# The last layer of a DCN cross kernel: row tails ahead of the sums, two row tiles through a DMA transpose, one semaphore for the last stores

## The chip, the cores and the metric

One core of a Trainium2 chip runs the kernel. Its engines are TensorE (PE in the profile, PEld for its weight loads), VectorE (DVE), ScalarE (ACT), GpSimd (POOL) and SyncE (SP), which here issues DMAs and waits. The metric is the time of one execution on the device in microseconds (us), lower is better; the number for a kernel is the median of its runs.

## The reference

```python
B, F, D, L = 4096, 26, 16, 6          # Din = 416
def reference(x0, ws, bs):            # x0 [4096, 416], ws [6, 416, 416], bs [6, 416], bf16
    x = x0
    for l in range(ws.shape[0]):
        x = x0 * (x @ ws[l] + bs[l]) + x
    return x
```

Six cross layers, each a 416x416 matrix product, an elementwise product with the input and a sum. Since every layer multiplies by the same x0, x after any layer is x0 times a running sum: x = x0 * (1 + sum over the layers of (x_l W_l + b_l)).

## The kernel before, in words

The 4096 rows are cut into four blocks of 1024 rows (`s`, size `SB`), each of two halves of 512 (`h`). Within a block the activations are kept transposed: features on the 128 partitions, rows along the free dimension. The 416 features are three chunks of 128 (`c`, `m`, `k`) and a tail of 32 columns.

PSUM holds the running sum of a block over all its layers: bank `3h + m` for half `h` and output chunk `m`, and banks 6 and 7 (`T_BANK`) for the tail. It is not reset between layers. `main` (mains) multiplies a 128-feature chunk of x with the weights, as four matmuls of 32 columns that run beside one another; `tail_rows` adds what the 32 tail features contribute, `tail_outs` makes the tail's own outputs. After each layer `leave` (L437, DVE) forms x = x0 * (PSUM + constant) for the next layer into `xT_sb`, where the constants (`cb_sb`) are one plus the summed biases. `leave_tail` does the same for the tail: ACT copies PSUM to `t32_sb` (L447), POOL multiplies (L460), and ACT and POOL make copies that the row-packed tail matmuls need (L424, L426).

`Plan` records every operation with what it reads and writes, in the order in which the Python loops name them. Each engine runs its operations in that order; where one needs a result of another engine or of a DMA, it waits on a semaphore. An operation that reads a PSUM bank is ordered behind earlier readers of that bank. Each DMA group has one semaphore, named by the `dma=` argument; a wait on it is for all DMAs of the group. Where an operation needs several semaphores, extra wait instructions stand ahead of it in its queue.

For blocks 0 to 2, `transpose_block` (L474) turns the finished block back with DMA transposes on SP's queue (L477, L482), and `store_block` (L484), called at L585 for `l == 3` of the next block, lets POOL place the tail columns (L488) and SP store the rows (L501).

The last layer of the last block (`s = 3`, `l = 5`) is computed the other way round, with rows on the partitions, so that no transposing is needed behind it. It has eight row tiles (`j`) of 128 rows, one PSUM bank each (`ROW_BANKS`, tile 0 in bank 6, 1 in 7, 2 to 7 in banks 0 to 5):

- `keep_sum` (L466) saves the running sums plus constant of layers 0 to 4 as bf16 into `sS_sb`, before the banks are taken over: half 0 on ACT, half 1 on ACT, ACT and DVE. `bt` and `st` (L588, L593, POOL) do that for the tail.
- `row_main` (L626) computes x W for a tile; tiles 0 to 3 "narrow", as four 32-column matmuls each, tiles 4 to 7 whole.
- `row_sums` (L636) adds the kept sums, turned by a multiplication with the identity.
- `row_tails` (L648) adds what the tail features and tail sums contribute, to all eight tiles at once, four tiles in each of two groups; for tiles 4 to 7 it is the first write of the bank.
- `finish` (L670) multiplies by x0 (`xr_sb`, loaded by rows): on DVE straight from PSUM (L674), or by an ACT copy (L681) and a POOL product (L685) for tiles 1 and 3.
- `store_rows` (L689) stores one or two tiles; six stores on SP's and ACT's queues, each with a semaphore of its own. SP then waits for all of them and for the earlier blocks' stores.

The order of the end: mains of tiles 0 to 3, sums of tiles 0 to 3, tails, `finish` of 0 to 3, and then main, sums and `finish` of each of 4 to 7.

Of the kernel before, what the change touches and what calls it, by code (L numbers as in the profile page):

```python
# [6 lines left out]
FP32 = mybir.dt.float32  # L7
ALU = mybir.AluOpType
# [110 lines left out]
def bass_standalone__dcn_v2_cross__recsys_kernel(  # L119
# [6 lines left out]
    B, D = x0.shape  # L126
    L = ws.shape[0]
    NC = 3
    DF = 128 * NC
    DR = D - DF  # L130
    assert DR == 32
    SB = 1024
    NS = B // SB
    H = SB // 2
# [5 lines left out]
    CH = range(NC)  # L140

    with ExitStack() as es:

        def sb(name, shape, dt=BF16):
            return es.enter_context(nc.sbuf_tensor(name, shape, dt))

        w_sb = sb("w_sb", [128, L, NC, D])
# [5 lines left out]
        xr_sb = sb("xr_sb", [128, JS, D])  # L153
        x0T_sb = sb("x0T_sb", [128, NC, B])
# [4 lines left out]
        sS_sb = sb("sS_sb", [128, NC, SB])  # L159
        st_sb = sb("st_sb", [128, G])  # L160
        f32_sb = sb("f32_sb", [128, 2, D], FP32)
        xo_sb = sb("xo_sb", [128, NS - 1, NC, SB])
        xot_sb = sb("xot_sb", [128, NS - 1, G])
        ot_sb = sb("ot_sb", [128, NS - 1, 2, 128])
# [16 lines left out]
        P = Plan()  # L181
# [4 lines left out]
        def bank(h, m):  # L186
            return NC * h + m


        def load(queue, dst, src, name, writes):  # L190
            P.add(queue, lambda e: e.dma_start(dst, src), writes=writes, dma=name)
# [76 lines left out]
            ), reads=[("ones",)], writes=[("u",)],  # L268
        )
        P.add("gpsimd", lambda e: e.memset(wc_sb[:, :, :], 0.0), writes=[("wc", "wt%d" % i) for i in range(3)])  # L270

        def replicate():
            for g, eng in ((1, "gpsimd"), (3, "scalar"), (2, "gpsimd")):
# [33 lines left out]
        def src_main(s, l):  # L307
            if l == 0:
                return x0T_sb, s * SB
            return xT_sb[:, l % 2], 0  # L310
# [116 lines left out]
                P.add(eng, fn, reads=[key], parts=[key + ("swapped",)], shifts=True)  # L427


        def leave(s, l, h, c):  # L430
            if l == L - 1:
                dst, key = xo_sb[:, s, c, h * H:(h + 1) * H], ("xo", s, c, h)
            else:
                dst, key = xT_sb[:, (l + 1) % 2, c, h * H:(h + 1) * H], ("xT", (l + 1) % 2, c, h)
            o = s * SB + h * H
            P.add(
                "vector", lambda e: e.scalar_tensor_tensor(  # L437
                    out=dst, in0=ps[:, bank(h, c), :], scalar=cb_sb[:, c, l:l + 1], in1=x0T_sb[:, c, o:o + H],
                    op0=ALU.add, op1=ALU.mult,
                ), reads=[("ps", bank(h, c)), ("cb",), ("x0T", s, c, h)], writes=[key],  # L440
            )
# [22 lines left out]
                swap(xt_sb[:, (l + 1) % 2], key, ("scalar", "gpsimd", "scalar", "gpsimd"))  # L464

        def keep_sum(h, c, eng):  # L466
            o, i, b = sS_sb[:, c, h * H:(h + 1) * H], ps[:, bank(h, c), :], cb_sb[:, c, L - 1:L]
            if eng == "scalar":
                fn = lambda e: e.activation(out=o, in_=i, func=ACTF.Identity, bias=b)  # L469
            else:  # L470
                fn = lambda e: e.tensor_scalar_add(o, i, b)
            P.add(eng, fn, reads=[("ps", bank(h, c)), ("cb",)], writes=[("sS", c, h)])

        def transpose_block(s):  # L474
            for c in CH:
# [76 lines left out]
        for s in range(NS):  # L552
            for l in range(L):
                ending = s == NS - 1 and l == L - 2
                if s == NS - 1 and l == L - 1:
                    break
                if s == 0 and l == 0:
                    for k in CH:
                        for part in range(2) if k == 0 else (None,):
                            for m in CH:  # L560
                                main(s, l, 0, m, k, part)
                        if k == 1:
                            tail_in()
                            bias_sums()
                    tail_rows(s, l, True)
                    for c in CH:
                        leave(s, l, 0, c)
                    tail_outs(s, l, False)
                else:
                    for m in CH:  # L570
                        for k in CH:
                            main(s, l, 0, m, k)
                    tail_rows(s, l, l == 0)
                    for c in CH:
                        leave(s, l, 0, c)
                    tail_outs(s, l, False)
                if s == 0 and l == 1:
                    corner(2, L, "wt2")
                leave_tail(s, l, not ending)
                if l == 2 and 0 < s < NS - 1:  # L580
                    place_tail(s + 1)
                if s == 0 and l == 0:
                    corner(1, 2, "wt1")
                if l == 3 and s > 0:
                    store_block(s - 1)  # L585
                if ending:
                    P.add(
                        "gpsimd", lambda e: e.tensor_tensor(  # L588
                            out=bt_sb[:, :], in0=cb_sb[:, NC, L - 1:L], in1=cb_sb[:, NC, L - 2:L - 1], op=ALU.subtract
                        ), reads=[("cb",)], writes=[("bt",)],  # L590
                    )
                    P.add(
                        "gpsimd", lambda e, t=t32_sb[:, l % 2, :]: e.tensor_scalar_add(st_sb[:, :], t, bt_sb[:, :]),  # L593
                        reads=[("t32", l % 2), ("bt",)], writes=[("st",)],
                    )
                    for c in CH:
                        keep_sum(0, c, "scalar")
                for m in CH:
                    for k in CH:
                        main(s, l, 1, m, k)  # L600
                    leave(s, l, 1, m)
                if ending:
                    for c in CH:
                        keep_sum(1, c, ("scalar", "scalar", "vector")[c])
            if s < NS - 1:
                transpose_block(s)
            if s < NS - 2:
                load_transposed(s + 2, 0, SB)
                load_last_columns(s + 2)
            if s == NS - 2:  # L610
                load("sync", xr_sb[:, :, :], x0_v[:, (NS - 1) * JS:NJ, :], "xr", [("xr",)])


        s, l = NS - 1, L - 1
        ROW_BANKS = (6, 7, 0, 1, 2, 3, 4, 5)
        src, off = src_main(s, l)
        srct, tkey = src_tail(s, l)

        def row_mm(pe, dst, lhsT, rhs, start, narrow):
# [6 lines left out]
        def row_main(j, start, narrow):  # L626
            b, h = ROW_BANKS[j], j // 4
            for k in CH:
                P.add(
                    "tensor", lambda pe, k=k: row_mm(  # L630
                        pe, ps[:, b, 0:D], src[:, k, off + j * 128:off + (j + 1) * 128], w_sb[:, l, k, :],
                        start and k == 0, narrow,
                    ), reads=[("w", l), src_key(s, l, k, h)], adds=[("ps", b)],
                )
# [34 lines left out]

        def finish(j, by_pool):  # L670
            b, jj = ROW_BANKS[j], (NS - 1) * JS + j
            if by_pool is None:
                P.add(
                    "vector", lambda e: e.tensor_tensor(  # L674
                        out=o_sb[:, jj, :], in0=ps[:, b, 0:D], in1=xr_sb[:, j, :], op=ALU.mult
                    ), reads=[("ps", b), ("xr",)], writes=[("ol", j)],
                )
                return
            t = f32_sb[:, by_pool, :]
            P.add(  # L680
                "scalar", lambda e: e.activation(out=t, in_=ps[:, b, 0:D], func=ACTF.Copy),  # L681
                reads=[("ps", b)], writes=[("f32", by_pool)],
            )
            P.add(
                "gpsimd", lambda e: e.tensor_tensor(out=o_sb[:, jj, :], in0=t, in1=xr_sb[:, j, :], op=ALU.mult),  # L685
                reads=[("f32", by_pool), ("xr",)], writes=[("ol", j)],
            )

        def store_rows(queue, a, b):  # L689
            ja = (NS - 1) * JS  # L690
            P.add(
                queue, lambda e: e.dma_start(out_v[:, ja + a:ja + b, :], o_sb[:, ja + a:ja + b, :]),
                reads=[("ol", j) for j in range(a, b)], writes=[("outl", a)], dma="outl%d" % a,
            )

        for j in range(4):
            row_main(j, True, True)
        for j in range(4):
            row_sums(j, True)
        row_tails()  # L700
        finish(0, None)
        finish(1, 0)
        finish(2, None)
        finish(3, 1)
        for j in range(4, 8):
            row_main(j, False, False)
            row_sums(j, False)
            finish(j, None)
        STORES = (("scalar", 2, 3), ("sync", 0, 2), ("sync", 4, 6), ("sync", 3, 4), ("scalar", 6, 7), ("sync", 7, 8))
        for queue, a, b in STORES:  # L710
            store_rows(queue, a, b)
        P.add("sync", None, reads=[("out", s) for s in range(NS - 1)] + [("outl", a) for _, a, _ in STORES])

        P.emit(nc, es)

# [27 lines left out]
```

## Time and profile before

| what | value |
|---|---|
| median of 3 runs | 128.45 us (127.77 to 128.56) |
| the profiled execution's own time | 128.46 us |
| its span, first to last instruction | 127.2 us |
| granted TensorE clock | 1.00 |
| busy: PE, DVE, ACT, POOL | 123.7, 99.7, 43.6, 38.8 us |
| one layer of a block, in the middle | about 4.9 us |
| the last layer, from its first main to the last product | 118.2 to 125.2 us |

The span is measured between the first and the last instruction of the program on the core; the run's time also holds what lies before and behind. Matmuls overlap one another, so a busy PE is a PE that always has something under way. All matmuls have the line L289, since one helper issues them; they are told apart by their tiles. A row of the timeline gives the start in us, the busy time in us, engine, line and operation, output and inputs, shapes, how many instructions it merges, and in brackets how long the engine was idle before it and what ended that. A row of a line's answer gives how often it ran, the least, median and greatest duration in ns, and for DMAs the time from issue to landing.

### The profile page before, as it was taken

Reading aid. Unit: us, or ns where it says so; the run is one execution under the profiler, and the core shown is the slowest. Engines: PE = TensorE matmul, PEld = TensorE weight load, DVE = VectorE, ACT = ScalarE, POOL = GpSimd, SP = SyncE. Lnnn points to the kernel's source line nnn. Section 1 sums busy time; section 2 is a strip of 40 time slices with the busy share of each in tenths; the row PEclk is TensorE's granted clock in tenths of the full one; section 3 lists DMA queues with packets and bytes.
Section 4 is the critical chain, followed back from the end, with each engine's and each line's share of the span. In section 5 each row is a group of like instructions: output and inputs, shape, how many; then the busy total and the mean of one; then the engine's idle time right before and its main releaser. Section 6 shows DMA issues by size and latency. Waiting matters only on the chain.

```text
span 127.2 us, 5308 instructions
## 1 busy us (share of the span) xinstructions
PE 123.7 (97%) x2414; PEld 65.1 (51%) x2414; DVE 99.7 (78%) x156; ACT 43.6 (34%) x95; POOL 38.8 (31%) x81
## 2 busy tenths in 40 slices
PE   7999999999999999999999999999999999999991
PEld 5754554554545545545545545545545545455660
DVE  2449779779779779779789788797797797797973
ACT  3324325225205225225204233243222252253820
POOL 6505324124104044054023142152221241351550
DMA  4998999010039693107028794108008870006117
GB/s 123 216 237 222 294 108 191 2 36 10 8 82 129 122 225 60 31 23 261 0 57 196 67 209 86 35 10 268 5 0 203 91 252 0 5 0 219 54 39 234
DMA packets 34438, 14.03 MB, mean 110 GB/s; under 512 B 25738, under 2 KB 34416, under 8 KB 34416
## 3 DMA queue, kind: packets, MB, share of 16 engines
q1 hardware_dynamic: 33376, 13.20, 48.4%
q10 hardware_dynamic: 1008, 0.49, 1.3%
q8 instruction: 19, 0.31, 1.0%
q14 instruction: 3, 0.02, 0.1%
q0 software_dynamic: 32, 0.01, 0.1%
HBM read 3.79 MB, written 3.41 MB: 57 GB/s over the span
## 4 chain that ended last, share of the span: by engine, by line
PE 97%; DVE 0%; issue 0%
PE ps L289 94%; PE ps L297 2%; PE ps L515 1%; DVE o_sb L674 0%
## 5 line engine op out<-in xcount | busy, mean ns | idle before, releaser
L437 DVE SCALAR_TENSOR_TENSOR xT_sb<-ps,cb_sb,x0T_sb 128x512 bf16<-128x512 f32 x120 | 80.9, 744 | 16.4 <-PE ps L289 16.4
L289 PE MATMUL ps<-xT_sb,w_sb 128*32 128x512 bf16 (+1 forms) x1596 | 84.2, 364 | 0.0
L289 PEld LDWEIGHTS ps<-xT_sb,w_sb 128*32 128x32 bf16 x1596 | 41.0, 97 | 37.1 <-issue 4.0
L447 ACT ACTIVATE t_sb<-ps,cb_sb 64x256 f32<-64x256 f32 x46 | 21.6, 469 | 57.2 <-PE ps L289 56.9
L460 POOL TENSOR_TENSOR xt_sb<-t_sb,x0t_sb 128x256 bf16<-128x256 f32 x20 | 13.4, 671 | 66.4 <-ACT t_sb L447 66.4
L424 ACT ACTIVATE xt_sb<-xt_sb 32x256 bf16<-32x256 bf16 x38 | 15.7, 414 | 15.1 <-POOL xt_sb L460 14.9
L289 PE MATMUL ps<-x0T_sb,w_sb 128*32 128x512 bf16 (+1 forms) x348 | 18.9, 364 | 0.0
L426 POOL COPY xt_sb<-xt_sb 32x256 bf16<-32x256 bf16 x38 | 14.9, 392 | 2.4
L437 DVE SCALAR_TENSOR_TENSOR xo_sb<-ps,cb_sb,x0T_sb 128x512 bf16<-128x512 f32 x18 | 12.1, 743 | 2.5 <-PE ps L289 2.5
L289 PEld LDWEIGHTS ps<-x0T_sb,w_sb 128*32 128x32 bf16 x348 | 8.9, 99 | 7.5 <-issue 0.8
L289 PE MATMUL ps<-xt_sb,wt_sb 32*128 32x512 bf16 (+1 forms) x152 | 11.6, 326 | 0.0
L289 PE MATMUL ps<-xt_sb,wc_sb 32*128 32x256 bf16 x76 | 7.3, 268 | 0.0
L289 PEld LDWEIGHTS ps<-xt_sb,wt_sb 32*128 32x128 bf16 x152 | 2.3, 92 | 8.1 <-DVE xT_sb L437 8.1
L289 PE MATMUL ps<-w_sb,xT_sb 128*32 128x416 bf16 (+1 forms) x60 | 5.1, 339 | 0.0
L460 POOL TENSOR_TENSOR xot_sb<-t_sb,x0t_sb 128x256 bf16<-128x256 f32 x3 | 2.0, 673 | 9.9 <-ACT t_sb L447 9.9
L674 DVE TENSOR_TENSOR o_sb<-ps,xr_sb 128x416 bf16<-128x416 f32 x6 | 3.4, 588 | 1.3 <-PE ps L289 1.0
L289 PEld LDWEIGHTS ps<-xt_sb,wc_sb 32*128 32x128 bf16 x76 | 3.9, 93 | 0.2
L297 PE MATMUL ps<-const-bfloat16-1.0 128*128 128x256 bf16 x14 | 3.1, 414 | 0.8 <-PEq L728 0.8
L525 DVE COPY x0T_sb<-ps 128x256 bf16<-128x256 bf16 x6 | 1.4, 287 | 2.6 <-PE ps L515 2.5
L469 ACT ACTIVATE sS_sb<-ps,cb_sb 128x512 bf16<-128x512 f32 x5 | 3.0, 690 | 0.0
L289 PEld LDWEIGHTS ps<-w_sb,xT_sb 128*32 128x32 bf16 (+1 forms) x60 | 2.3, 97 | 1.4 <-issue 0.2
L685 POOL TENSOR_TENSOR o_sb<-f_sb,xr_sb 128x416 bf16<-128x416 f32 x2 | 1.9, 972 | 2.9 <-ACT f_sb L681 2.9
(43 smaller groups left out, 29.4 us busy)
## 6 DMA issues: line engine op xcount, KB each, us to landing
out_dram<-o_sb SPq DMA_DIRECT2D x2, 832.0 KB, 4.3
w_sb<-in_ws_dram SPq DMA_DIRECT2D x5, 312.0 KB, 4.0
out_dram<-o_sb SPq DMA_DIRECT2D x2, 416.0 KB, 3.2
xr_sb<-in_x_dram SPq DMA_DIRECT2D x1, 832.0 KB, 5.0
wt_sb<-in_ws_dram SPq DMA_DIRECT2D x4, 104.0 KB, 3.4
out_dram<-o_sb SPq DMA_DIRECT2D x2, 208.0 KB, 2.2
w_sb<-in_ws_dram SPq DMA_DIRECT2D x3, 104.0 KB, 3.4
xin_sb<-in_x_dram ACTq DMA_DIRECT2D x1, 208.0 KB, 3.2
```

The lines of the kernel that those rows point to most:

```text
L289: return pe.matmul(dst, lhsT=lhsT, rhs=rhs, start=start, stop=True, skip_group_check=True, tile_position=pos,)
L297: ins = pe.matmul(ps[:, 7, 0:256], lhsT=const[:, 0:128], rhs=const, start=True, stop=True)
L424: fn = lambda e, d=dst, s=src: e.activation(out=d, in_=s, func=ACTF.Copy)
L426: fn = lambda e, d=dst, s=src: e.tensor_copy(out=d, in_=s)
L437: "vector", lambda e: e.scalar_tensor_tensor(out=dst, in0=ps[:, bank(h, c), :], scalar=cb_sb[:, c, l:l + 1], in1=x0T_sb[:, c, o:o + H], op ...
L447: "scalar", lambda e, p=p, h=h: e.activation(out=dst[p, :], in_=ps[p, T_BANK[h], 0:G], func=ACTF.Identity, bias=cb_sb[p, NC, l:l + 1]), re ...
L460: "gpsimd", lambda e: e.tensor_tensor(out=dst, in0=t, in1=x0t_sb[:, s, 0, :], op=ALU.mult),
L469: fn = lambda e: e.activation(out=o, in_=i, func=ACTF.Identity, bias=b)
L515: ins = pe.transpose(out=psT[:, b, j * 128:(j + 1) * 128], in_=xin_sb[:, 2 * i + j, c * 128:(c + 1) * 128], identity=ident[:, :],)
L525: "vector", lambda e, d=dst, s=src: e.tensor_copy(out=d, in_=s),
L674: "vector", lambda e: e.tensor_tensor(out=o_sb[:, jj, :], in0=ps[:, b, 0:D], in1=xr_sb[:, j, :], op=ALU.mult), reads=[("ps", b), ("xr",)], ...
L685: "gpsimd", lambda e: e.tensor_tensor(out=o_sb[:, jj, :], in0=t, in1=xr_sb[:, j, :], op=ALU.mult),
```

## The change

It has four parts.

1. All six last stores share one semaphore, so that SP's final wait is one; the wait for the earlier blocks' stores moves ahead of the last stores. The stores are cut and ordered otherwise (`STORES`).
2. In the last layer, `row_tails` follows the mains of tiles 0 to 3 and stands ahead of the sums; the sums of tiles 2 and 3 are whole matmuls, not narrow ones.
3. Tiles 0 and 1 have no sums any more. They are computed as x0*(x W + b) + x: z = x0*b on POOL ahead of time, x transposed back by one DMA transpose on SP's queue into `xl_sb`, y = z + xl (POOL for tile 0, DVE for tile 1), p = x0 * PSUM, and the output p + y. For this, `leave` of layer 4 in the last block writes x in an order in which a tile's three chunks lie side by side (`xj`). The tail columns of y are zero, since the tails still come with their sums.
4. The kept sums of half 0 cover only tiles 2 and 3, all of them are on ACT, tile 0 is finished by ACT and POOL and tile 1 by DVE, and the store of block 2 is issued a layer earlier.

```diff
+        P.add("gpsimd", lambda e: e.memset(y_sb[:, :, DF:D], 0.0), writes=[("yz",)])
...
+        xj = xT_sb[:, (L - 1) % 2, :, :].rearrange("p c n -> p (c n)").rearrange("p (j c f) -> p j c f", c=NC, f=128)
...
         def leave(s, l, h, c):
+            if s == NS - 1 and l == L - 2:
+                o, js = s * SB + h * H, slice(4 * h, 4 * h + 4)
+                P.add(
+                    "vector", lambda e: e.scalar_tensor_tensor(
+                        out=xj[:, js, c, :], in0=ps[:, bank(h, c), :].rearrange("p (j f) -> p j f", f=128),
...
         def keep_sum(h, c, eng):
-            o, i, b = sS_sb[:, c, h * H:(h + 1) * H], ps[:, bank(h, c), :], cb_sb[:, c, L - 1:L]
+            lo = 0 if h else 256
+            o, i, b = sS_sb[:, c, h * H + lo:(h + 1) * H], ps[:, bank(h, c), lo:H], cb_sb[:, c, L - 1:L]
...
+        def transpose_first():
+            P.add(
+                "sync", lambda e: e.dma_start_transpose(
+                    xl_sb.rearrange("p j (c f) -> p (j c) f", c=NC), xj[:, 0:2, :, :].rearrange("p j c f -> p (j c f)")
+                ), reads=[("xT", (L - 1) % 2, c, 0) for c in CH], writes=[("xl",)], dma="xl",
+            )
...
                     for c in CH:
                         leave(s, l, 0, c)
+                    if ending:
+                        transpose_first()
                     tail_outs(s, l, False)
...
-                if l == 3 and s > 0:
+                if s > 0 and l == (3 if s < NS - 1 else 2):
                     store_block(s - 1)
+                if s == NS - 1 and l == 3:
+                    for j in range(2):
+                        P.add(
+                            "gpsimd", lambda e, j=j: e.tensor_tensor(
+                                out=z_sb[:, j, :], in0=xr_sb[:, j, 0:DF], in1=bl_sb[:, :], op=ALU.mult
+                            ), reads=[("xr",), ("bl",)], writes=[("z", j)],
+                        )
...
                 if ending:
                     for c in CH:
-                        keep_sum(1, c, ("scalar", "scalar", "vector")[c])
+                        keep_sum(1, c, "scalar")
+                    for j in range(2):
+                        P.add(
+                            ("gpsimd", "vector")[j], lambda e, j=j: e.tensor_tensor(
+                                out=y_sb[:, j, 0:DF], in0=z_sb[:, j, :], in1=xl_sb[:, j, :], op=ALU.add
+                            ), reads=[("z", j), ("xl",)], writes=[("y", j)],
+                        )
...
                 load("sync", xr_sb[:, :, :], x0_v[:, (NS - 1) * JS:NJ, :], "xr", [("xr",)])
+                load("sync", bl_sb[:, :], bs[L - 1:L, 0:DF].to_broadcast([128, DF]), "bl", [("bl",)])
...
         def finish(j, by_pool):
             b, jj = ROW_BANKS[j], (NS - 1) * JS + j
+            o = o_sb[:, jj, :]
+            mid, key = (p_sb[:, j, :], ("p", j)) if j < 2 else (o, ("ol", j))
+
+            def add_x(eng):
+                if j < 2:
+                    P.add(
+                        eng, lambda e: e.tensor_tensor(out=o, in0=mid, in1=y_sb[:, j, :], op=ALU.add),
+                        reads=[("p", j), ("y", j), ("yz",)], writes=[("ol", j)],
+                    )
...
-                reads=[("ol", j) for j in range(a, b)], writes=[("outl", a)], dma="outl%d" % a,
+                reads=[("ol", j) for j in range(a, b)], writes=[("outl", a)], dma="outl",
...
         for j in range(4):
             row_main(j, True, True)
-        for j in range(4):
-            row_sums(j, True)
         row_tails()
-        finish(0, None)
-        finish(1, 0)
-        finish(2, None)
-        finish(3, 1)
+        finish(0, 0)
+        finish(1, None)
+        for j in range(2, 4):
+            row_sums(j, False)
+            finish(j, (None, 1)[j - 2])
         for j in range(4, 8):
             row_main(j, False, False)
             row_sums(j, False)
             finish(j, None)
-        STORES = (("scalar", 2, 3), ("sync", 0, 2), ("sync", 4, 6), ("sync", 3, 4), ("scalar", 6, 7), ("sync", 7, 8))
+        STORES = (
+            ("scalar", 1, 3), ("sync", 4, 6), ("scalar", 0, 1), ("sync", 6, 7), ("scalar", 3, 4), ("sync", 7, 8),
+        )
+        P.add("sync", None, reads=[("out", s) for s in range(NS - 1)])
         for queue, a, b in STORES:
             store_rows(queue, a, b)
-        P.add("sync", None, reads=[("out", s) for s in range(NS - 1)] + [("outl", a) for _, a, _ in STORES])
+        P.add("sync", None, reads=[("outl", a) for _, a, _ in STORES])
```

After the change the engines' own orders at the end are: PE mains 0 to 3, tails, sums 2 and 3, then main and sums of 4 to 7; DVE y1, p1, its sum o1, and the products of tiles 2, 4, 5, 6, 7; POOL st, y0, p0, its sum o0, the product of tile 3; ACT six kept sums, the copies of tiles 0 and 3, and its three stores; SP the transpose, the waits for the earlier blocks, and its three stores.

More of the change, by code (lines that the diff above doesn't have):

```diff
@@ L161, in bass_standalone__dcn_v2_cross__recsys_kernel @@
         f32_sb = sb("f32_sb", [128, 2, D], FP32)
+        xl_sb = sb("xl_sb", [128, 2, DF])
+        bl_sb = sb("bl_sb", [128, DF])
+        z_sb = sb("z_sb", [128, 2, DF], FP32)
+        y_sb = sb("y_sb", [128, 2, D], FP32)
+        p_sb = sb("p_sb", [128, 2, D], FP32)
         xo_sb = sb("xo_sb", [128, NS - 1, NC, SB])
@@ L427, in swap @@
                 P.add(eng, fn, reads=[key], parts=[key + ("swapped",)], shifts=True)
+        xj = xT_sb[:, (L - 1) % 2, :, :].rearrange("p c n -> p (c n)").rearrange("p (j c f) -> p j c f", c=NC, f=128)
         def leave(s, l, h, c):
+            if s == NS - 1 and l == L - 2:
[3 more added lines that the diff above has]
+                        out=xj[:, js, c, :], in0=ps[:, bank(h, c), :].rearrange("p (j f) -> p j f", f=128),
+                        scalar=cb_sb[:, c, l:l + 1], in1=x0T_sb[:, c, o:o + H].rearrange("p (j f) -> p j f", f=128),
+                        op0=ALU.add, op1=ALU.mult,
+                    ), reads=[("ps", bank(h, c)), ("cb",), ("x0T", s, c, h)], writes=[("xT", (l + 1) % 2, c, h)],
+                )
+                return
             if l == L - 1:
@@ L611, in bass_standalone__dcn_v2_cross__recsys_kernel @@
                 load("sync", xr_sb[:, :, :], x0_v[:, (NS - 1) * JS:NJ, :], "xr", [("xr",)])
+                load("sync", bl_sb[:, :], bs[L - 1:L, 0:DF].to_broadcast([128, DF]), "bl", [("bl",)])
         s, l = NS - 1, L - 1
         ROW_BANKS = (6, 7, 0, 1, 2, 3, 4, 5)
-        src, off = src_main(s, l)
         srct, tkey = src_tail(s, l)
@@ L630, in row_main @@
                     "tensor", lambda pe, k=k: row_mm(
-                        pe, ps[:, b, 0:D], src[:, k, off + j * 128:off + (j + 1) * 128], w_sb[:, l, k, :],
+                        pe, ps[:, b, 0:D], xj[:, j, k, :], w_sb[:, l, k, :],
                         start and k == 0, narrow,
@@ L674, in finish @@
                     "vector", lambda e: e.tensor_tensor(
-                        out=o_sb[:, jj, :], in0=ps[:, b, 0:D], in1=xr_sb[:, j, :], op=ALU.mult
-                    ), reads=[("ps", b), ("xr",)], writes=[("ol", j)],
+                        out=mid, in0=ps[:, b, 0:D], in1=xr_sb[:, j, :], op=ALU.mult
+                    ), reads=[("ps", b), ("xr",)], writes=[key],
                 )
+                add_x("vector")
                 return
@@ L684, in finish @@
             P.add(
-                "gpsimd", lambda e: e.tensor_tensor(out=o_sb[:, jj, :], in0=t, in1=xr_sb[:, j, :], op=ALU.mult),
-                reads=[("f32", by_pool), ("xr",)], writes=[("ol", j)],
+                "gpsimd", lambda e: e.tensor_tensor(out=mid, in0=t, in1=xr_sb[:, j, :], op=ALU.mult),
+                reads=[("f32", by_pool), ("xr",)], writes=[key],
             )
+            add_x("gpsimd")
         def store_rows(queue, a, b):
@@ L708, in bass_standalone__dcn_v2_cross__recsys_kernel @@
             finish(j, None)
-        STORES = (("scalar", 2, 3), ("sync", 0, 2), ("sync", 4, 6), ("sync", 3, 4), ("scalar", 6, 7), ("sync", 7, 8))
+        STORES = (
+            ("scalar", 1, 3), ("sync", 4, 6), ("scalar", 0, 1), ("sync", 6, 7), ("scalar", 3, 4), ("sync", 7, 8),
+        )
+        P.add("sync", None, reads=[("out", s) for s in range(NS - 1)])
         for queue, a, b in STORES:
             store_rows(queue, a, b)
-        P.add("sync", None, reads=[("out", s) for s in range(NS - 1)] + [("outl", a) for _, a, _ in STORES])
+        P.add("sync", None, reads=[("outl", a) for _, a, _ in STORES])
         P.emit(nc, es)
```

## The prediction, as it was put on record

> **What bounds the kernel now.** I read the chain that ended last first, then the last 10 us of the timeline engine by engine, then the waits of SP's queue, then the rows that could price the new operations. The chain:
>
> ```profile
> by line: PE ps L289 93.7%; PE ps L297 2.5%; PE ps L515 1.1%; DVE o_sb L674 0.5%; issue 0.1%
> ...
> 5.35 119.24 PE ps L289 x2287
> 124.59 0.02 issue
> 124.62 0.59 DVE o_sb L674
> ```
>
> TensorE (PE) carries everything up to 124.59 us; one VectorE (DVE) product of the last row tile and one store follow. The granted clock is 1.00 throughout, so the throttle takes no part. The change touches the last layer of the last block, so its worth is read there:
>
> ```profile
> 119.82 0.70 PE L289 MATMUL ps<-w_sb,xT_sb 128*32 128x416 bf16 x12
> 120.35 0.84 PE L289 MATMUL ps<-ident,sS_sb 128*32 128x128 bf16 x48
> 121.12 0.35 PE L289 MATMUL ps<-wt_sb,xt_sb 32*128 32x416 bf16 x4
> 121.31 0.18 PE L289 MATMUL ps<-ident,st_sb 32*128 32x32 bf16 x4
> 121.34 0.34 PE L289 MATMUL ps<-wt_sb,xt_sb 32*128 32x416 bf16 x4
> 121.51 0.18 PE L289 MATMUL ps<-ident,st_sb 32*128 32x32 bf16 x4
> ```
>
> The reader sees the order mains, sums of four tiles, tails; no tile is complete before the tails end, so the first evacuation starts late:
>
> ```profile
> 119.83 0.74 DVE L471 TENSOR_SCALAR sS_sb<-ps,cb_sb 128x512 bf16<-128x512 f32 x1
> 121.56 3.65 DVE L674 TENSOR_TENSOR o_sb<-ps,xr_sb 128x416 bf16<-128x416 f32 x6 [0.99 <-PE ps L289]
> ...
> 124.62 0.59 DVE L674 TENSOR_TENSOR o_sb<-ps,xr_sb 128x416 bf16<-128x416 f32 x1
> ```
>
> DVE idles 0.99 us and then does six products. Behind one another they start 0.50 us apart (121.56, 122.07, 122.57), though one lasts 0.59; the last three start 0.695 apart (123.23, 123.92, 124.62), which is PE's time for a tile (three 416-wide mains, three 128-wide sums). So DVE has 0.19 us of room a tile at the end; PE sets the pace. Behind the last product: store issued at 125.24, last of its semaphore counts at 127.08 (1.84 later), and then
>
> ```profile
> SPq L109 <- DMA out_dram<-o_sb: 1.4, 3, 0.6
> ```
>
> SP's final waits: in the trace's records of SP, the instruction that sees the last store ends at 127.10, and two more waits, long fulfilled, end the span at 127.23. The profiled execution took 128.46 us, so 1.23 lies around the span. The median of the three runs is 128.45: the same.
>
> **The change, part by part.** Times are on the trace of before.
>
> *One semaphore.* The two spare waits behind the last store go: 127.10 to 127.23, a gain of 0.13. The waits for earlier blocks move ahead of the last stores in SP's queue; the last of those stores, issued at 114.73, had landed by 119.14 and now goes out a layer earlier, so they pass. 0.13 is taken, bounds 0.10 to 0.13.
>
> *Block 2's store at l=2.* Its POOL copy (0.40) and SP issue move from 114.3 to about 109.4. Its transposes had landed by 101.0, and POOL's idle before the next L460 is 3.30 us. Nothing waits for it: 0.
>
> *z, bl, the memset of y.* Two POOL products of 128x384 go at 114.3, where the copy stood. POOL's rows give 0.67 for 256 elements and 0.97 for 416, so 0.91 each; they end at 116.1, ahead of L460 at 117.56. The broadcast load queues behind xr (landed 104.85). The memset of 64 elements sits behind the 1.24 us memset of wc (ends 3.71); POOL then waits for a load until 4.26. All 0; if the cover were gone it would be 0.4 (z) and nothing else.
>
> *ACT takes all kept sums.* The three of half 0 shrink from 512 to 256 columns. The 512-wide row lasts 0.69 and repeats every 0.57; the 256-wide L447 lasts 0.47 and repeats every 0.48 without overlap, 0.36 with the overlap of the 512-wide ones. I take 0.36 (same form as the latter). Starts 117.51, 117.87, 118.22; half 1 then follows its leaves (ends 118.60, 119.26, 119.91): 118.66, 119.31, 119.97, and the last ends at 120.67, semaphore 120.69. By 0.48 it would be 120.81. On DVE it ended at 120.57.
>
> *PE.* The last narrow mains start at 120.17. The step from column groups to row groups costs 0.31 after 512-wide matmuls (110.22 to 110.53) and 0.15 after 128-wide ones (120.97 to 121.12), so 0.27 after 416: first tails at 120.44, second 0.19 later at 120.63. But the second start the banks of tiles 5 and 7, and the bank of tile 7 is what the last kept sum reads: a new wait on ACT, until 120.69, and about 0.11 for PE to move (two waits in its queue stand 0.11 apart at 11.82 and 11.93): 120.80. Queued behind it are all sums and mains. From second tails to the next group was 0.31 before (121.31 to 121.62): sums of tiles 2 and 3 from 121.11, six at 0.055, main of tile 4 at 121.44 against 121.63. PE gains 0.19; bounds 0.06 (late ACT) and 0.35 (no wait). Tile 7 is complete at 124.40, tile 1 about 0.42 after its tails start (121.34 to 121.74 had 0.40): 121.22.
>
> *The transpose.* SP issues it at 117.97, when the last half-0 leave (117.94) is done; SP has nothing queued but this. For SBUF to SBUF the rows are
>
> ```profile
> L477 SPq DMA_TRANSPOSE o_sb<-xo_sb x9: 1245/1307/1312, 35.7 to 96.9; - x9
> DMA to landing us min/median/max: 2.7/2.8/4.5
> ...
> L482 SPq DMA_TRANSPOSE ot_sb<-xot_sb x3: 1253/1612/2331, 39.7 to 98.2; - x3
> DMA to landing us min/median/max: 2.4/2.8/3.5
> ```
>
> Eight 128-blocks and two blocks land alike when first in the queue: 2.73 to 2.77, and 2.42 at best. The 4.5 belongs to the third of a row with more loads behind it. Six blocks alone: 2.75 taken, bounds 2.4 and 4.5. Landed at 120.72.
>
> *DVE.* It loses the kept sum (0.74, at a time when it is free) and two products move: tile 0 goes to ACT and POOL, tile 1 stays on DVE with two operations more. y1 starts at 120.75. For SBUF-only f32 sums there is no DVE row; the nearest is L674, 0.59 for 416 from PSUM, spaced 0.50. Below: the 0.50 scaled to 384, 0.46; above: POOL's 0.97 for the same shape. I take 0.475 for y1 and 0.59 for the last sum o1, nearest to L674. Product p1: 121.25 (PE's tile 1) to 121.84. o1 needs p1 of its own engine: the memset pair at the start shows 0.14 from end to start: 121.98. Then tiles 2, 4, 5, 6, 7 every 0.50: 122.48, 122.98, 123.48, 123.98, 124.48. PE's 124.40 for tile 7 is covered; DVE and PE end level, and DVE is 0.08 the later. The product ends at 125.07 instead of 125.21: a gain of 0.14.
>
> *POOL and ACT.* Tile 0 complete at 120.86, ACT's copy 0.52, well before POOL is done with y0: 120.79 to 121.70; p0 to 122.67; 0.10 for its own semaphore (as 118.39 to 118.49); o0 to 123.74; tile 3's product to 124.70; its store on ACT's queue at 124.73, landing by 126.6 to 126.9 (before: 1.78 to 2.24). It is 0.36 ahead of the last store.
>
> *End.* Store at 125.09, plus 1.84, plus 0.02: span 126.95 against 127.23, 0.28 less (0.14 from DVE, 0.13 from the waits, the rest rounding). With 1.23 around it: 128.18, say 128.2.
>
> **The rule that speaks against it.** No row of before shows DVE reading two SBUF tensors beside a POOL operation: L437 and L674 read one from PSUM, and POOL's L685 lasts 0.972 beside them both times. The Trainium skill, "SBUF — State Buffer", "Who interferes with whom", says that a DVE instruction with two SBUF inputs and a POOL instruction that reads SBUF exclude each other for the whole instruction. By that rule y1 and o1 would take turns with y0, p0, o0 and the time would be that of rivals 1 or 2 instead of 128.2. No run here shows it yet.
>
> **Rivals.**
> 1. *DVE and POOL take turns, o1 ahead of p0.* y1 and y0 are released by the same landing. DVE follows a semaphore in 0.02 to 0.03 us, POOL in 0.07, so y1 goes first, to 121.30; y0 to 122.21; o1 to 122.80; p0 to 123.77; o0 to 124.84; tile 3 to 125.77. DVE's last product ends at 125.30, but tile 3's store, issued at 125.80, lands at 127.65: span 127.68, time 128.9. For it: five new operations with two SBUF sources each inside 4 us; against it: no row.
> 2. *The same, p0 ahead of o1.* o1 waits until p0 ends at 123.13, ends at 123.73; products 2 to 7 from 123.63, the last ends at 126.22, lands at 128.08: span 128.11, time 129.35. It decides as soon as o1 is held past 122.1, where DVE's room is gone. This and rival 1 end on the slower side.
> 3. *The transpose lands late* (4.5): y1 at 122.5 holds all DVE products behind it by 1.75: 129.9. Against it: nothing else is in the queue.
> 4. *The lower bounds all hold* (no ACT wait, landing in 2.42, own-engine wait 0.04): PE gives tile 7 at 124.25, end 126.7: 127.95. Against: the leave of half 1 ends at 119.91 and the kept sum cannot be earlier.
>
> **How the numbers follow.** Forecast (no turns) 0.46, its own range 127.9 to 128.5: the late ACT sum (+0.12) and the scatter of the three runs (127.77 to 128.56) lie in it. Rival 1: 0.24. Rival 2: 0.18. Rival 3: 0.04. Rival 4: 0.08. The likeliest gives 128.2. The range for 8 in 10 must take in both turn-taking cases, so 127.8 to 129.4. About 1% (1.3 us) is what a measurement of this kernel can tell from no change; faster by that (under 127.2) is none of the cases: 0.02; slower by that (over 129.7) is rival 3 and a worse rival 2: 0.05; within: 0.93.
>
> **What would show it.** Right: the sums row after the tails; second tails at about 120.8 with ACT as releaser; y1 near 120.75; DVE without a gap from y1 to the end and the last product near 124.5; one final wait on SP. Turns: y0 or o1 longer than 1.0 or 0.7 us, or starting late after their releaser. Rival 3: y1 after 121.5 with the transpose as releaser. The forecast is wrong if the last store is not tile 7's, or if the last DVE product starts after 125.

## The result, and the profile after

The changed kernel takes 128.71 us (median of 22 runs, 128.24 to 129.50); the kernel before, run beside it, 128.11 us (22 runs, 127.77 to 129.07). The ratio is 1.0047, with a 95% interval of 1.0031 to 1.0062: 0.6 us slower. That lies within 1% and inside the range on record, but on the other side of no change than the 0.3 us of gain that the forecast worked out. The forecast's 128.2 us stood on three runs of the kernel before with a median of 128.45; on the 128.11 measured here the same gain gives 127.83, so the miss is 0.88 us and only by luck looks like 0.5.

The profiled execution of the changed kernel took 129.37 us, of which 128.1 is span. Its layers began 0.22 us later than in the trace of before, from the first layer on (DVE's first `leave` starts at 8.77 us against 8.55). The change isn't the cause: in the nine kernels below that are built from the changed one, the last layer begins anywhere from 117.41 to 118.54 us. So all times below that are called "from the last layer's start" count from the first main matmul of the last layer (118.24 us in before, 118.46 in after). On this scale the span ends at 8.99 before and at 9.63 after: 0.64 later, close to the 0.60 by which the medians differ.

The chain that ended last, in the kernel after (start, length, what):

```profile
by line: PE ps L295 86.4%; PE ps L303 2.5%; DMA xl_sb<-xT_sb 2.0%; DVE o_sb L725 1.9%; DVE xT_sb L442 1.6%; PE ps L541 1.1%; DVE y_sb L642 1.0%; DVE o_sb L719 0.6%; DVE p_sb L725 0.4%; issue 0.1%; DVEq L109 0.0%
...
5.34 110.72 PE ps L295 x2075
...
118.19 2.52 DMA xl_sb<-xT_sb
...
120.73 0.02 DVEq L109
...
120.80 1.31 DVE y_sb L642
122.11 0.51 DVE p_sb L725
...
122.64 0.75 DVE o_sb L719
123.39 2.49 DVE o_sb L725 x5
```

Before, PE carried the chain to 124.59 us. Now PE leaves it at 116.07, and the last 10 us go through DVE's leaves of x, the transpose, y1, p1, o1 and five products; from y1 on DVE has no gap over 0.04. DVE has become the bound. The timeline shows why (start, busy time, engine, line, operation; in brackets the idle time before it and what ended that):

```profile
120.78 0.91 POOL L642 TENSOR_TENSOR y_sb<-z_sb,xl_sb 128x384 f32<-128x384 f32 x1 [1.14 <-DMA xl_sb<-xT_sb]
120.80 1.31 DVE L642 TENSOR_TENSOR y_sb<-z_sb,xl_sb 128x384 f32<-128x384 f32 x1 [0.66 <-DMA xl_sb<-xT_sb]
...
121.71 1.24 POOL L737 TENSOR_TENSOR p_sb<-f_sb,xr_sb 128x416 f32<-128x416 f32 x1
...
122.03 0.58 DVE L725 TENSOR_TENSOR p_sb<-ps,xr_sb 128x416 f32<-128x416 f32 x1
...
122.64 0.75 DVE L719 TENSOR_TENSOR o_sb<-p_sb,y_sb 128x416 bf16<-128x416 f32 x1
...
123.02 1.29 POOL L719 TENSOR_TENSOR o_sb<-p_sb,y_sb 128x416 bf16<-128x416 f32 x1
123.31 2.57 DVE L725 TENSOR_TENSOR o_sb<-ps,xr_sb 128x416 bf16<-128x416 f32 x5
...
124.28 0.97 POOL L737 TENSOR_TENSOR o_sb<-f_sb,xr_sb 128x416 bf16<-128x416 f32 x1
```

The same operation on the same shape lasts 0.91 on POOL and 1.31 on DVE. It isn't idle time: no bracket stands ahead of o1, and the table of DVE's waits has no row for POOL there. The instruction has begun and is held inside its own duration. Nor do the two work beside each other: in the records y0 ends at 121.690 and y1 at 122.105, 0.415 later, and the pattern repeats with o1, which ends 0.45 after p0, and with o0, which ends 0.92 after o1. DVE's products, with one input in PSUM, show nothing of the kind: p1 takes 0.58 though POOL's p0 runs through all of it.

PE did what the change asks of it:

```profile
120.67 0.35 PE L295 MATMUL ps<-wt_sb,xt_sb 32*128 32x416 bf16 x4
...
121.06 0.36 PE L295 MATMUL ps<-wt_sb,xt_sb 32*128 32x416 bf16 x4
...
121.37 0.51 PE L295 MATMUL ps<-ident,sS_sb 128*128 128x128 bf16 x6
121.71 0.69 PE L295 MATMUL ps<-w_sb,xT_sb 128*128 128x416 bf16 x3
```

From the last layer's start the second tails begin at 2.60 (before 3.10), the mains of tile 4 at 3.25 (before 3.39) and PE's last matmul at 5.98 (before 6.12). That 0.14 is of no use, because DVE's last product starts 0.87 after PE's last matmul, where it started 0.26 after it before. SP's final waits for the stores are one now (waited for: total, times, longest):

```profile
SPq L109 <- DMA out_dram<-o_sb: 1.6, 1, 1.6
```

The 0.64 us splits into four, each a difference of after and before on the scale of the last layer: DVE's last product starts 0.47 later (6.85 against 6.38); its store is issued another 0.04 later after it (SP is still at tile 6's store); the store takes 2.08 (2.09 in the expectations below) instead of 1.84 to land, 0.25; and 0.03 instead of 0.15 passes from there to the end of the span, −0.11. The sum is 0.65, with rounding.

### The profile page after: what moved, and what is told of

It is laid out like the page before. It is cut to its first block, busy times and chain, and to the rows that moved or that the text cites. A ratio compares the mean times of both kernels' runs of the same rounds, so it can differ in the third digit from the quotient of the medians.

```text
span 128.1 us, 5231 instructions
## 1 busy us (share of the span) xinstructions
PE 123.8 (97%) x2372; PEld 64.8 (51%) x2372; DVE 100.7 (79%) x157; ACT 43.9 (34%) x96; POOL 43.2 (34%) x86
## 4 chain that ended last, share of the span: by engine, by line
PE 90%; DVE 6%; DMA 2%; issue 0%; DVEq 0%
PE ps L295 86%; PE ps L303 2%; DMA xl_sb<-xT_sb 2%; DVE o_sb L725 2%; DVE xT_sb L442 2%; PE ps L541 1%; DVE y_sb L642 1%; DVE o_sb L719 1%; DVE p_sb L725 0%; DVEq L109 0%
## 5 line engine op out<-in xcount | busy, mean ns | idle before, releaser
L488 ACT ACTIVATE sS_sb<-ps,cb_sb 128x256 bf16<-128x256 f32 (+1 forms) x6 | 3.2, 579 | 0.0
L303 PEld LDWEIGHTS ps<-const-bfloat16-1.0 128*128 128x128 bf16 x14 | 2.0, 145 | 1.5 <-issue 0.8
```

Source lines behind the costliest of these rows:

```text
L303: ins = pe.matmul(ps[:, 7, 0:256], lhsT=const[:, 0:128], rhs=const, start=True, stop=True)
```

## The experiments

The theory formed on these lines: DVE and POOL take turns whenever a DVE operation with two SBUF inputs meets a POOL operation that reads SBUF. Its rivals: a sum of two SBUF tensors is simply slow on DVE; two engines that read the same tensors hinder each other; any POOL work hinders DVE. Each end below is the end of the span from the last layer's start (before 8.99, after 9.63). Six kernels (`pool_other`, `pool_memset`, `no_tile0`, `kept_dve`, `fewer_stores`, `last_alone`) were timed once each, so only their traces are read.

### One semaphore alone

Run `one_sem`, on the kernel before:

```diff
-                ... dma="outl%d" % a,
+                ... dma="outl",
...
+        P.add("sync", None, reads=[("out", s) for s in range(NS - 1)])
         for queue, a, b in STORES:
             store_rows(queue, a, b)
-        P.add("sync", None, reads=[("out", s) for s in range(NS - 1)] + [("outl", a) for _, a, _ in STORES])
+        P.add("sync", None, reads=[("outl", a) for _, a, _ in STORES])
```

> The kernel before with part 1 alone: one semaphore for the six last stores, the wait for the earlier blocks' stores ahead of them. Both theories (taking turns on SBUF; the new sums being slow by themselves) leave this part out of the loss: the two spare waits of 0.13 us go, nothing else moves. Expected 0.1 us under the kernel before, last DVE product as before, 6.38 us after the first main of the last layer.

Measured: 128.11 us (12 runs) against 128.29 (29 runs), ratio 0.9989 (0.9966 to 1.0012); end 8.91, 0.08 less. In the run times that can't be told from nothing; in the trace the two spare waits are gone, and nothing else on the path has moved by more than 0.03.

### The tails ahead of the sums alone

Run `tails_first`, on the kernel before, with `row_tails` ahead of whole sums of tiles 0 to 3:

```diff
-        for j in range(4):
-            row_sums(j, True)
         row_tails()
-        finish(0, None)
-        finish(1, 0)
-        finish(2, None)
-        finish(3, 1)
+        for j in range(4):
+            row_sums(j, False)
+            finish(j, (None, 0, None, 1)[j])
```

> The kernel before with part 2 alone: tails ahead of the sums, all four sums whole, no transposed tiles, own semaphores. DVE has no operation with two SBUF inputs here, so by both theories its products keep their 0.58 us and 0.50 spacing. PE does the same work: tails 0.12 us later than right behind the mains because of the step from 416-wide mains, sums as long as narrow ones. Expected within 0.1 us of the kernel before; if the order of tails and sums itself were the cause of the loss, 0.3 us or more slower.

Measured: 128.26 us, ratio 1.000 (0.9976 to 1.0023), end 9.01. PE's last matmul starts at 6.29, 0.17 later than before (the expectation had 0.12 later tails for the step from the wide mains to the tails) and 0.31 later than in the changed kernel, since here two more tiles' sums stand behind the tails. The last store lands in 1.70 instead of 1.84; why is not shown. The order alone neither costs nor gives. What it gave PE in the changed kernel came with the two tiles that have no sums at all.

### DVE first

Run `y1_first`, the changed kernel with one dependence more: y0 waits for y1.

```diff
-                    for j in range(2):
+                    for j in (1, 0):
...
-                            ), reads=[("z", j), ("xl",)], writes=[("y", j)],
+                            ), reads=[("z", j), ("xl",)] + ([] if j else [("y", 1)]), writes=[("y", j)],
```

> The changed kernel with one wait more: POOL's y0 starts when DVE's y1 is done, nothing else. Turns theory: y1 takes 0.56 us instead of 1.31, since POOL is idle beside it; o1 still meets y0 or p0 and is stretched to some 0.9; DVE's last product starts 0.5 to 0.6 earlier than in the changed kernel, POOL's chain ends 0.4 later, and the time is 0.2 to 0.4 us under the changed kernel's. Slow-sum theory (a DVE sum of f32 and bf16 from SBUF takes 1.3 us by itself): y1 stays at 1.3, y0 starts 1.3 later, and the time is 0.3 us or more above the changed kernel's.

Its timeline:

```profile
119.81 0.56 DVE L642 TENSOR_TENSOR y_sb<-z_sb,xl_sb 128x384 f32<-128x384 f32 x1 [0.66 <-DMA xl_sb<-xT_sb]
...
120.45 0.91 POOL L642 TENSOR_TENSOR y_sb<-z_sb,xl_sb 128x384 f32<-128x384 f32 x1 [1.79 <-DVE y_sb L642]
...
121.14 0.67 DVE L719 TENSOR_TENSOR o_sb<-p_sb,y_sb 128x416 bf16<-128x416 f32 x1
...
121.33 1.32 POOL L737 TENSOR_TENSOR p_sb<-f_sb,xr_sb 128x416 f32<-128x416 f32 x1
```

y1 alone takes 0.56 instead of 1.31. So the sum isn't slow on DVE; it was held. The holding goes on further down: o1 begins at 121.14, while y0 still runs, and ends 0.45 after y0 (it takes 0.67, less than the 0.9 expected, since y0 had only 0.22 left); p0 begins at 121.33, while o1 runs, and lasts 1.32. DVE's last product starts at 6.26 instead of 6.85, and the end is at 9.31: 0.32 less than after, 0.32 more than before. The run times give 128.38 us, ratio to before 1.0017 (0.9991 to 1.0043). The last store to land is now that of tile 3 (issued 7.28, landed 9.28), which comes from POOL: this is rival 1 of the prediction, whose end on this scale was 9.44 (127.68 less 118.24).

### All of tile 0 on DVE

Run `tile0_dve`, on the changed kernel:

```diff
-                            ("gpsimd", "vector")[j], lambda e, j=j: e.tensor_tensor(
+                            "vector", lambda e, j=j: e.tensor_tensor(
...
-        finish(0, 0)
+        finish(0, None)
```

> The changed kernel with all three operations of tile 0 (y0, p0, o0) on DVE; POOL has only tile 3's product, from about 121.9 to 122.9. Turns theory: y0 and y1 take 0.56 each, 0.475 apart; the one sum that meets tile 3's product is stretched (to as much as 1.1) and that product is 0.97 or stretched itself; the other sum is 0.6. DVE has eleven operations in a row, so the time is 0.4 to 0.8 us above the changed kernel's. Slow-sum theory: y0 and y1 take 1.3 each, both sums 0.75, and the time is 2 us above.

```profile
120.43 1.03 DVE L642 TENSOR_TENSOR y_sb<-z_sb,xl_sb 128x384 f32<-128x384 f32 x2 [0.66 <-DMA xl_sb<-xT_sb]
...
121.99 0.59 DVE L719 TENSOR_TENSOR o_sb<-p_sb,y_sb 128x416 bf16<-128x416 f32 x1
122.14 1.28 POOL L737 TENSOR_TENSOR o_sb<-f_sb,xr_sb 128x416 bf16<-128x416 f32 x1 [2.86 <-ACT f_sb L733]
...
123.12 0.75 DVE L719 TENSOR_TENSOR o_sb<-p_sb,y_sb 128x416 bf16<-128x416 f32 x1
```

With POOL quiet, both y together take 1.03. POOL then has only tile 3's product, and even that one meets both final sums: it begins inside the first and lasts 1.28 (0.97 undisturbed); the second begins inside it and lasts 0.75 instead of 0.59. Three more operations cost DVE more than the turns did: 129.87 us (4 runs), ratio 1.0120 (1.0074 to 1.0165), end 10.40. In the trace that is 0.77 above the changed kernel, at the upper edge of what was expected; by the two ratios to the kernel before it is some 0.9, a little beyond it.

### What POOL must do to hold DVE

On the kernel with DVE first, POOL gets one unused operation more, released by the same landing as y1: in one kernel (`pool_other`) a product of tensors that y1 doesn't touch, in the other (`pool_memset`) a memset of about the same length.

```diff
+        scr_sb = sb("scr_sb", [128, DF], FP32)
...
+                    P.add(
+                        "gpsimd", lambda e: e.tensor_tensor(
+                            out=scr_sb[:, :], in0=x0T_sb[:, 0, 0:DF], in1=x0T_sb[:, 1, 0:DF], op=ALU.mult
+                        ), reads=[("xl",)], writes=[("scr",)],
+                    )
```

> The kernel in which y0 waits for y1, plus one POOL product added that reads two other SBUF tensors (two chunks of x0T, 128x384) into scratch and is released by the same landing as y1. It adds work that the output does not use. If the turns are about the port that POOL and DVE share, any POOL read of SBUF holds y1: POOL goes first by some 20 ns as in the changed kernel, and y1 takes 1.3 us again. If it is about the tensors that y0 and y1 have in common (z, xl, y), y1 stays at 0.56.

```profile
120.07 0.91 POOL L642 TENSOR_TENSOR scr_sb<-x0T_sb 128x384 f32<-128x384 bf16 x1 [1.15 <-DMA xl_sb<-xT_sb]
120.09 1.30 DVE L648 TENSOR_TENSOR y_sb<-z_sb,xl_sb 128x384 f32<-128x384 f32 x1 [0.67 <-DMA xl_sb<-xT_sb]
```

```diff
+        scr_sb = sb("scr_sb", [128, 960], FP32)
...
+                    P.add("gpsimd", lambda e: e.memset(scr_sb[:, :], 0.0), reads=[("xl",)], writes=[("scr",)])
```

> The same place, but POOL's added operation is a memset of 128x960 f32 (0.9 us, by the 1.24 us of the 1344-column memset at the start), which reads nothing; its output is not used. If only POOL's reads exclude DVE's second SBUF input, y1 takes 0.56. If any POOL work does, y1 takes 1.3.

```profile
120.84 0.90 POOL L641 MEMSET scr_sb<- 128x960 f32 x1 [1.12 <-DMA xl_sb<-xT_sb]
120.88 0.56 DVE L644 TENSOR_TENSOR y_sb<-z_sb,xl_sb 128x384 f32<-128x384 f32 x1 [0.66 <-DMA xl_sb<-xT_sb]
```

These two lines against the two above settle it: beside 0.91 us of POOL work that reads SBUF y1 takes 1.30, though no tensor is common; beside 0.90 us that only writes it takes 0.56. Common tensors and "any POOL work" are out. Every POOL operation that held a DVE sum here reads two SBUF tensors; one that reads a single one was not run beside a DVE sum. The operations added push POOL's chain back, so the whole times (129.10 and 129.36 us) say nothing more.

### The changed kernel without POOL's part of tile 0

Run `no_tile0`. It leaves out y0, p0, o0 and the store of tile 0, so it shows what the turns cost and is no kernel to use:

```diff
-                    for j in range(2):
+                    for j in (1,):
...
-        finish(0, 0)
...
-            ... ("sync", 4, 6), ("scalar", 0, 1), ("sync", 6, 7), ...
+            ... ("sync", 4, 6), ("sync", 6, 7), ...
```

> The changed kernel without tile 0's y0, p0, o0 on POOL and its store, so tile 0's rows of the output are left out; ACT has one copy less, PE is untouched. Turns theory: y1 takes 0.56, p1 starts when PE has tile 1 (3.0 us after the first main of the last layer), o1 is 0.6 and free, DVE's last product starts at 6.2 to 6.25 when PE has tile 7, as the forecast's sum had it, and the end is at 8.65 to 8.85 instead of 9.63. If DVE's chain were too long for another reason, the last product would stay near 6.85.

```profile
120.32 0.56 DVE L642 TENSOR_TENSOR y_sb<-z_sb,xl_sb 128x384 f32<-128x384 f32 x1 [0.66 <-DMA xl_sb<-xT_sb]
...
121.64 0.59 DVE L719 TENSOR_TENSOR o_sb<-p_sb,y_sb 128x416 bf16<-128x416 f32 x1
...
122.15 2.65 DVE L725 TENSOR_TENSOR o_sb<-ps,xr_sb 128x416 bf16<-128x416 f32 x5
```

This prices the turns on DVE. p1 starts at 3.04 instead of 3.57, 0.53 earlier; o1 is 0.16 shorter; the five products take 0.08 more, since PE now paces some of them. 0.53 + 0.16 − 0.08 = 0.61, and DVE's last product indeed starts 0.62 earlier (6.23). The end is at 8.66; the forecast's, on this scale, was 8.71 (126.95 less 118.24).

### The last kept sum on DVE

Run `kept_dve`, on the kernel with DVE first:

```diff
-                        keep_sum(1, c, "scalar")
+                        keep_sum(1, c, ("scalar", "scalar", "vector")[c])
```

> The kernel in which y0 waits for y1, with the last kept sum back on DVE as in the kernel before, so that the second tails no longer wait for ACT. Measured from the first main of the last layer, the second tails start at 2.45 to 2.5 us instead of 2.57, and PE is 0.1 earlier. DVE does the kept sum until 2.56 and starts y1 then, 0.2 later than in that kernel; since DVE sets the end there, the time is 0.1 to 0.2 us more, not less.

```profile
120.14 0.74 DVE L490 TENSOR_SCALAR sS_sb<-ps,cb_sb 128x512 bf16<-128x512 f32 x1
...
120.88 0.56 DVE L642 TENSOR_TENSOR y_sb<-z_sb,xl_sb 128x384 f32<-128x384 f32 x1
```

The second tails start at 2.43 instead of 2.60 and PE's last matmul at 5.79 instead of 5.98. So the wait for ACT's last kept sum that the prediction added to PE is real and costs 0.19. The expected 0.2 us on DVE did not come: the kept sum lay in DVE's wait for the transpose, and y1 starts at 2.34 as without it. The end stays at 9.31, since tile 3's store from POOL sets it and not, as the expectation had it, DVE: PE's wait was off the path.

### Where the last store's 2.08 us go

Two kernels that leave stores out of the changed one. The first is `fewer_stores`:

```diff
-            ("scalar", 1, 3), ("sync", 4, 6), ("scalar", 0, 1), ("sync", 6, 7), ("scalar", 3, 4), ("sync", 7, 8),
+            ("sync", 4, 6), ("sync", 6, 7), ("scalar", 3, 4), ("sync", 7, 8),
```

> The changed kernel without the stores of tiles 0, 1 and 2, so those rows of the output are left out. DVE and POOL are as in the changed kernel. If the last store's 2.09 us from issue to landing (1.84 before) come from stores queued ahead of it, it falls to 1.7 to 1.85 and the span by 0.25 to 0.35; if the wait is SP's own, it stays at 2.09.

Measured: end 9.58, the last landing still 2.08 after its issue. The expected fall didn't come: the stores of tiles 0 to 2 are not what holds the last one. The four stores that are left still land 0.31 to 0.34 apart. So next the two just ahead of the last were left out instead (`last_alone`):

```diff
-            ("scalar", 1, 3), ("sync", 4, 6), ("scalar", 0, 1), ("sync", 6, 7), ("scalar", 3, 4), ("sync", 7, 8),
+            ("scalar", 1, 3), ("sync", 4, 6), ("scalar", 0, 1), ("sync", 7, 8),
```

> The changed kernel without the stores of tiles 3 and 6, so those rows of the output are left out. DVE and POOL are as in the changed kernel, but for SP's free queue. In the run without the stores of tiles 0 to 2 the last four stores still landed 0.32 us apart, so if the last store's 2.09 us come from the ones just ahead of it, it falls to 1.75 to 1.85 here and the end comes 0.3 us earlier, measured from the first main of the last layer (9.63 in the changed kernel, 9.3 here). If the latency is the store's own, it stays at 2.09 and the end moves by 0.05 at most.

SP's final wait in it, and from its table of DMAs SP's store of one tile, which is here the last one (KB, us from issue to landing):

```profile
SPq L109 <- DMA out_dram<-o_sb: 1.3, 1, 1.3
...
out_dram<-o_sb SPq DMA_DIRECT2D x1, 104.0 KB, 1.7
```

The last store lands 1.68 after its issue and the end falls to 9.17, 0.46 less. That is more than the 0.3 expected: 0.41 from the landing and 0.05 from the issue. In the changed kernel, with DVE late, the stores of tiles 3, 6 and 7 are issued within 0.7 us (125.28, 125.42 and 125.97) and land one after another.

### A version without the turns

What the runs say should be kept was put together in `one_tile`: only tile 0 goes through the transpose, with all three operations on DVE; tile 1 has sums again and is finished by ACT and POOL; the last kept sum is on DVE; the tails stay ahead and the semaphore is one.

```diff
-            lo = 0 if h else 256
+            lo = 0 if h else 128
...
-        finish(0, 0)
-        finish(1, None)
-        for j in range(2, 4):
+        finish(0, None)
+        for j in range(1, 4):
             row_sums(j, False)
-            finish(j, (None, 1)[j - 2])
+            finish(j, (0, None, 1)[j - 1])
...
-            ("scalar", 1, 3), ("sync", 4, 6), ("scalar", 0, 1), ("sync", 6, 7), ("scalar", 3, 4), ("sync", 7, 8),
+            ("scalar", 0, 1), ("sync", 1, 3), ("sync", 4, 6), ("scalar", 3, 4), ("scalar", 6, 7), ("sync", 7, 8),
```

> A version drawn from the runs: only tile 0 goes through the DMA transpose, with y0, p0, o0 on DVE; tile 1 keeps its sums and goes by ACT and POOL as before, so POOL has two products alone; the last kept sum is back on DVE; tails ahead of the sums and one semaphore as in the changed kernel. Turns theory: y0 takes 0.56, POOL being idle; o0 (at 3.5 us after the first main of the last layer) is free or holds POOL's first product by 0.4, which nothing waits for. PE completes tile 7 at 6.15 to 6.2 (kept_dve had 6.02, plus one sum of 0.165), DVE's last product starts at 6.2, the end is at 8.65 to 8.8 against 8.99 in the kernel before and 8.91 with one semaphore alone: 0.2 to 0.3 us under the kernel before. Rival: the transposed tile costs more than it saves in any form; then the end is at 8.9 or later.

```profile
120.24 0.54 DVE L642 TENSOR_TENSOR y_sb<-z_sb,xl_sb 128x384 f32<-128x384 f32 x1
...
121.32 0.59 DVE L719 TENSOR_TENSOR o_sb<-p_sb,y_sb 128x416 bf16<-128x416 f32 x1
121.68 2.00 POOL L737 TENSOR_TENSOR o_sb<-f_sb,xr_sb 128x416 bf16<-128x416 f32 x2 [2.52 <-ACT f_sb L733]
```

Both sums on DVE run at full speed: y0 has POOL idle beside it, and o0 had begun 0.36 before POOL's first product, which took 1.06 instead of 0.97. The end is at 8.56, 0.43 before the kernel before, better than expected, in one profile. The run times don't carry that: 127.94 us (12 runs, 127.22 to 128.54 but for one of 129.27) against 128.05 (17 runs), ratio 0.9996 (0.9965 to 1.0027). The scatter of the runs is three times 0.4 us. That this version beats the kernel before is not shown; that it undoes the loss of the change is, since its interval lies below the changed kernel's (1.0031 to 1.0062).

## Why the prediction was wrong, point by point

**The step that failed** is the price of y1 and o1: "I take 0.475 for y1 and 0.59 for the last sum o1, nearest to L674", and with it the choice of the case without turns ("Forecast (no turns) 0.46") over the two with turns (0.42 together). Undisturbed the two last 0.56 and 0.59, as no_tile0 and y1_first show, so the row was near enough. What failed was taking a row of an operation with one source in PSUM for one with both in SBUF, beside a POOL that reads SBUF: they measured 1.31 and 0.75. The bounds beside that sentence (0.46 to 0.97) didn't hold y1 either, since an operation that waits for its turn carries the other engine's time in its own. On the path this was worth 0.62 us (no_tile0). The sign that the prediction had named for turns came: o1 took more than 0.7.

The mechanism was that of the rivals, and the rule weighed there was right: the Trainium skill, "SBUF — State Buffer", "Who interferes with whom", says that a DVE instruction with two SBUF inputs contends with a POOL instruction that reads SBUF, and not with one that only writes it. The traces agree: 1.31 and 1.30 beside POOL's reads, 0.56 beside a POOL that only writes. The prediction had this rule and five such operations within 4 us for the turns and, in its own words, "against it: no row"; that no row of before showed turns either was no reason to give the case without them the largest share.

**The order of the turns** was wrong as well. "DVE follows a semaphore in 0.02 to 0.03 us, POOL in 0.07, so y1 goes first": POOL began at 120.780 and DVE at 120.799. y1 needs two results, and its second wait is an instruction of its own in DVE's queue (the `DVEq L109` piece of the chain), so DVE was 0.09 behind the landing. That this instruction is what put DVE behind is read from the records, not tested. Whoever began first went through undisturbed (POOL's y0 in 0.91, DVE's first sum in tile0_dve in 0.59); where a wait puts y1 ahead, the end is 0.32 earlier (y1_first). Of rival 2, p0 ahead of o1 came true; its end on this scale, 9.87, was not quite reached (9.63). With POOL first, y0 ended at 3.23 instead of rival 2's 3.97, and p0 at 4.49 instead of 4.89, so DVE's last product ended 0.55 sooner than in rival 2; the later store gave 0.30 of that back. (The rivals' own sums have two slips of 0.05 or less: after y0 at 122.21 a p0 of 0.97 ends at 123.18 and not 123.13, and tile 3 after o0 at 124.84 ends at 125.81 and not 125.77. Neither decides anything.)

**The last store** was taken at 1.84 as before and took 2.08; together with SP's 0.04 this is 0.28 of the 0.64. No step of the prediction asked what a late DVE does to the distance of the last stores. last_alone shows that it is the stores of tiles 3 and 6 just ahead.

**Right:** the spare waits (−0.13 expected, −0.11 measured); z, the broadcast load, the memset and block 2's store at 0 (from the last layer's start nothing before the transpose has moved); the second tails at 2.56, measured 2.60, with the wait for ACT; mains of tile 4 at 3.20, measured 3.25; the transpose's landing, 2.75 expected, 2.52 measured. **Smaller than taken:** the wait for its own engine ahead of o1, 0.14, measured 0.03. With no turns the working as a whole held: 8.71 against 8.66 in no_tile0. So, counted from no_tile0, the gain of about 0.33 us that the change would have had without turns was turned into a loss by 0.62 us of turns on DVE and 0.35 us at the last store (landing 2.08 instead of 1.77, issue 0.04 later).

## What to carry to other kernels

Before work is split between DVE and POOL to run side by side, count the SBUF inputs of the DVE operation: with two, and a POOL operation that reads SBUF (here always two tensors), the split is no split, and the loss appears as a longer operation, here never as a wait. Give POOL such work while DVE reads PSUM (tile 3's product in the changed kernel took 0.97 beside DVE's 0.58), or leave it out, as in the last experiment. At a kernel's end, price the last store with what is queued just ahead of it, not alone.

## What the runs showed of the hardware

- A DVE sum that is held needs most of its own time after the release: y1 ended 0.42 after POOL's operation (after, pool_other) and 0.56 is its whole length, so only about 0.14 of it was hidden.
- POOL is held in the same way: tile 3's product lasts 0.97 undisturbed (after) and 1.28 where it begins inside a DVE sum (tile0_dve).
- A DVE product with one input in PSUM isn't held: p1 took 0.58 beside POOL's p0 (after) and 0.59 with POOL idle (no_tile0).
- The DMA transpose of six blocks of 128 from SBUF to SBUF occupied SP for 1.23 us and landed 2.52 after its issue.
- Stores of one row tile (104 KB) landed 1.68 after their issue when the store ahead had been issued 0.93 earlier (last_alone), and 0.31 to 0.34 apart from one another when they followed closely (after, fewer_stores).
